# Feed-forward: weight conversions dealt over other steps, and accumulators evicted ahead of g's casts

## The chip, the cores and the metric

The kernel runs on one core of one Trainium2 chip. The metric is the device time of one execution in microseconds (us). Three runs of the kernel before took 407.21, 407.16 and 403.54 us; the median is 407.16.

## What is computed

Three layers follow each other: an attention with a local band and 32 global tokens (4 batches, 8 heads), a mixture of 8 experts with soft dispatch, and a feed-forward. The feed-forward, which the change touches, is

```
n_tokens, d_model, d_ff = (2304, 512, 2048)

def _moe2_ref(x, w_in, w_out) -> np.ndarray:
    h = x @ w_in
    g = h - np.tanh(h)
    return (g @ w_out).astype(np.float32)
```

Its input x is the output of the experts, a combination of 32 slots per token, so the kernel computes h from the combination weights and from a small matrix M (slots times w_in), with one matmul per 128 columns of d_ff. The weights w_in and w_out arrive as 64-bit words and are turned into 32-bit floats on the chip. The output has 17 tiles of 128 rows by 512 columns.

## The kernel before

**Steps.** The feed-forward is a list of 48 steps (L1116, from PHASES, L51). A step takes one chunk fc of 128 of the 2048 columns of d_ff and a group of six or five output tiles. The groups are tiles 0 to 5, 6 to 11 and 12 to 16; they are gone through with chunks 0 to 7 (steps 0 to 7, 8 to 15, 16 to 23) and then again with chunks 8 to 15 (steps 24 to 31, 32 to 39, 40 to 47). A sum over eight chunks is called a half: the accumulators of a group are evicted from PSUM once at the end of its first half (`keep_part`, L1178, on ScalarE) and once at the end of its second, where the two halves are added and written out (`emit_out`, L1184). A step of a group of five tiles (16 to 23 and 40 to 47) has 15 matmuls, the others 18.

**The matmuls of a step** (`ff`, L1167). Each tile takes three matmuls of 512 columns: the high half of g by the high half of the weight (L1174), the high half of g by the low half of the weight (L1175), the low half of g by the high half of the weight (L1176). So the second matmul of a step needs the low weight half `wlo[fc]` and the third the low half of g.

**g of a step, two steps ahead.** In step i the kernel makes g of step i + 2, in two parts (columns of the first three tiles, then of the others). One part goes from engine to engine:

- `g_head` (L1127): the h matmul on TensorE into one of two PSUM banks (L1133). The two banks take turns, so an h matmul must wait until the second tail of the part before the last has read its bank.
- `g_square` (L1138): u = h * h on ScalarE (L1140).
- `g_tail0` and `g_tail1` (L1144, L1148): two VectorE operations, h = (u - 2.5) * h (L1146), the first tail, and g = u * h (L1150), the second tail.
- `g_hi` (L1155): the high cast of g on ScalarE (L1157).
- `g_lo` (L1159): the low half, g minus its high cast, on GpSimd (L1161).

Each engine runs its instructions in the order in which the program issues them (`tc.manual_schedule`, L640). In the loop (L1332 to L1400) that order is, for part 0 and then part 1 of step i:

```
g_tail0(i + 2, part)
g_tail1(i + 2, part)
ff(i, tiles)
if part == 0: g_head(i + 2, 1); g_square(i + 2, 1)
if part == 0 and parts(i + 3) == 1: g_head(i + 3, 0); g_square(i + 3, 0)
g_hi(i + 2, part); g_lo(i + 2, part)
if part and parts(i + 3) > 1: g_head(i + 3, 0); g_square(i + 3, 0)
if last and i < len(steps) - 1: the evictions of the tiles of this part
```

So there is one h matmul in the middle of a step (for part 1 of step i + 2) and one at its end (for part 0 of step i + 3), and on ScalarE the high cast of part 0 stands behind the square of part 1. At the end of a half, in steps 7, 15 and 23, three evictions follow the high cast of part 0, and three (two) more follow the first square of the next step.

**Conversions.** A chunk of w_out (numbers 3 to 15) or w_in (numbers 24 to 31 stand for w_in's chunks 8 to 15) is turned from 64-bit words into floats by four operations: the head on ScalarE (`f32_head`, L531), then on VectorE the shift (L535), the high-word operation (L540) and the low-word operation (L545), from `f32_tail` (L533). A chunk of w_out then takes the high cast on ScalarE (L1036) and the low subtract on GpSimd (L1037), its low half. The chunks of w_out go through two conversion buffers in turn (`cv`, even and odd chunks), so the head of a chunk waits until the low subtract of the chunk two before it has read the buffer. `conv_ops` (L1026) gives a chunk's operations 0 to 5: nothing, shift, high-word, low-word, high cast, low subtract; `win_ops` (L618) gives the first four of a chunk of w_in.

**Where they stand before.** The table JOBS (L45) names the chunk of a step. Its head is issued in the middle of the step before (L1385 to L1391). Operation 1 follows the second tail of part 0, operation 2 the first tail of part 1, operation 3 the second tail of part 1 (L1342 to L1348), and operations 4 and 5 stand at the end of the step (L1398). Chunks 3 to 7 are converted in steps 1 to 5, each two steps ahead of the step that first uses it.

**M.** Two blocks of M are computed inside the loop, in steps 13 and 19 (MB, L49): `m_rows` (L1079) after the matmuls of part 0, `m_parts` (L1094) after those of part 1. Both take an h bank, so in these two steps the second h matmul takes the bank of the h matmul before it.

**Loads.** The raw chunks are loaded by `load_late` (L811), called at the top of each step (L1333) as long as a count that follows from JOBS allows and a buffer is free.

## Time and profile before

| What | Value |
|---|---|
| median of three runs | 407.16 us |
| the profiled execution | 406.85 us |
| its span, first to last instruction | 405.1 us |
| mean granted TensorE clock | 0.993 of full speed |
| TensorE busy | 382.9 us, 95% of the span |
| VectorE, ScalarE, GpSimd busy | 276.2, 218.2, 209.7 us |
| chain that ended last, on TensorE | 76% of the span |

A row of the timeline gives the start of an instruction in us from the start of the span, its duration in us, engine, line, operation, output <- input, shape, and in brackets how long its engine was idle before it and what ended that. PE is TensorE and PEld its weight loads, DVE VectorE, ACT ScalarE, POOL GpSimd. Matmuls overlap: from one start to the next is less than a duration. Names of buffers are of little use, since buffers are reused under old names (`slot`, `k_w`, `pg` are places in memory); the lines say what is done.

### The profile page before, as it was taken

Reading aid. Unit: us, or ns where it says so; the run is one execution under the profiler, and the core shown is the slowest. Engines: PE = TensorE matmul, PEld = TensorE weight load, DVE = VectorE, ACT = ScalarE, POOL = GpSimd, SP = SyncE. Lnnn points to the kernel's source line nnn. Section 1 sums busy time; section 2 is a strip of 40 time slices with the busy share of each in tenths; the row PEclk is TensorE's granted clock in tenths of the full one; section 3 lists DMA queues with packets and bytes.
Section 4 is the critical chain, followed back from the end, with each engine's and each line's share of the span. In section 5 each row is a group of like instructions: output and inputs, shape, how many; then the busy total and the mean of one; then the engine's idle time right before and its main releaser. Section 6 shows DMA issues by size and latency. Waiting matters only on the chain.

```text
span 405.1 us, 10230 instructions
## 1 busy us (share of the span) xinstructions
PE 382.9 (95%) x3767; PEld 279.6 (69%) x3767; DVE 276.2 (68%) x833; ACT 218.2 (54%) x542; POOL 209.7 (52%) x275
## 2 busy tenths in 40 slices
PE   7889889989999899999999999999989999999994
PEld 3677667766787433336877786786868888888873
DVE  4577698766476526449998886787879997555541
ACT  2677666865766202248655645566575645345330
POOL 3676576665564010016866444455575668347441
PEclk9999999999999999999999999999999999999998
DMA  6899999999768989999303101003100003002104
GB/s 182 264 401 317 321 335 268 357 334 294 266 183 270 332 254 418 416 420 385 111 0 105 53 1 53 0 4 94 60 2 2 0 28 129 0 2 113 44 2 138
DMA packets 33834, 70.43 MB, mean 174 GB/s; under 512 B 3824, under 2 KB 10736, under 8 KB 33776
## 3 DMA queue, kind: packets, MB, share of 16 engines
q1 hardware_dynamic: 33632, 69.56, 50.3%
q8 instruction: 32, 0.52, 0.5%
q14 instruction: 26, 0.21, 0.2%
q10 hardware_dynamic: 144, 0.13, 0.1%
HBM read 65.22 MB, written 4.46 MB: 172 GB/s over the span
## 4 chain that ended last, share of the span: by engine, by line
PE 76%; issue 6%; POOL 5%; DVE 4%; DMA 3%; ACT 3%; SPq 2%; DVEq 0%; POOLq 0%
PE a L1175 13%; PE a L1176 13%; PE a L1174 13%; PE sc L248 7%; PE a L971 4%; PE a L1010 4%; PE h L1133 4%; PE X L281 3%; PE ptp L269 3%; SPq L104 2%; PE gsc L430 2%; POOL q L210 2%; PE xTp L311 2%; PE ps L344 1%; DVE slot L1150 1%
## 5 line engine op out<-in xcount | busy, mean ns | idle before, releaser
L1161 POOL TENSOR_TENSOR slot<-slot 128x384 fp32r<-128x384 f32 x96 | 98.7, 1031 | 83.5 <-ACT slot L1157 79.8
L1174 PE MATMUL a<-slot 128*128 128x512 f32 x272 | 106.9, 393 | 1.3 <-ACT v_w L1182 0.7
L1176 PE MATMUL a<-slot 128*128 128x512 f32 x272 | 107.8, 396 | 0.0
L1175 PE MATMUL a<-slot 128*128 128x512 f32 x272 | 107.5, 395 | 0.0
L1146 DVE SCALAR_TENSOR_TENSOR h<-slot,h 128x384 f32<-128x384 f32 x96 | 51.5, 537 | 38.7 <-ACT slot L1140 38.4
L1157 ACT CAST slot<-slot 128x384 fp32r<-128x384 f32 x96 | 47.6, 496 | 49.5 <-DVE slot L1150 49.0
L1140 ACT ACTIVATE slot<-h 128x384 f32<-128x384 f32 x96 | 45.3, 473 | 34.5 <-PE h L1133 33.9
L1174 PEld LDWEIGHTS a<-slot 128*128 128x128 f32 x272 | 51.1, 188 | 14.2 <-ACT v_w L1182 1.5
L1176 PEld LDWEIGHTS a<-slot 128*128 128x128 f32 x272 | 51.0, 188 | 11.4
L1175 PEld LDWEIGHTS a<-slot 128*128 128x128 f32 x272 | 51.0, 188 | 9.3 <-POOL slot L1037 1.0
L1150 DVE TENSOR_TENSOR slot<-slot,h 128x384 f32<-128x384 f32 x96 | 50.8, 529 | 8.0 <-DVE h L1146 0.5
L258 ACT ACTIVATE sm<-sm,mb 128x128 f32<-128x128 f32 x128 | 41.2, 396 | 15.5 <-DVE mb L254 15.2
L248 PE MATMUL sc<-k,q 128*64 128x128 f32 x512 | 39.0, 294 | 4.9 <-POOL q L210 3.8
L210 POOL TENSOR_SCALAR v<-v 32x1300 f32<-32x1300 f32 (+5 forms) x40 | 34.2, 855 | 13.9 <-PE xgp L475 11.4
L248 PEld LDWEIGHTS sc<-k,q 128*64 128x64 f32 x512 | 33.3, 208 | 11.1 <-POOL q L210 5.9
L210 POOL TENSOR_SCALAR q<-q 64x256 f32<-64x256 f32 x62 | 27.5, 444 | 20.5 <-issue 11.0
L254 DVE CUSTOM_DVE_ANT_0 sm<-sc,mask 128x128 f32<-128x128 f32 x128 | 30.2, 284 | 10.9 <-PE sc L248 9.7
L1037 POOL TENSOR_TENSOR slot<-k_w,slot 128x512 fp32r<-128x512 f32 x16 | 20.7, 1296 | 32.5 <-ACT slot L1036 32.3
L1133 PE MATMUL h<-slot 128*128 128x384 f32 x96 | 32.4, 339 | 0.8 <-DVE slot L1150 0.6
L1133 PEld LDWEIGHTS h<-slot 128*128 128x128 f32 x96 | 17.9, 188 | 12.0 <-DVE slot L1150 5.9
L281 PE MATMUL X<-v,pt 128*32 128x65 f32 x1024 | 22.1, 223 | 1.4 <-issue 1.4
L281 PEld LDWEIGHTS X<-v,pt 128*32 128x32 f32 x1024 | 16.5, 109 | 7.2 <-issue 6.1
(239 smaller groups left out, 526.2 us busy)
## 6 DMA issues: line engine op xcount, KB each, us to landing
slot<-in_w_dram SPq DMA_DIRECT2D x55, 512.0 KB, 7.6
slot<-in_w_out_dram SPq DMA_DIRECT2D x9, 512.0 KB, 4.8
slot<-in_w_in_dram SPq DMA_DIRECT2D x16, 256.0 KB, 6.5
k<-in_k_dram SPq DMA_DIRECT2D x7, 576.0 KB, 7.8
q<-in_q_dram SPq DMA_DIRECT2D x15, 256.0 KB, 5.4
out_dram<-o SPq DMA_DIRECT2D x15, 256.0 KB, 2.1
slot<-in_w_in_dram SPq DMA_DIRECT2D x7, 512.0 KB, 10.0
v<-in_v_dram SPq DMA_DIRECT2D x8, 390.0 KB, 5.5
```

The costliest lines, as they stand in the source:

```text
L210: G.tensor_scalar(out=o, in0=i, scalar1=0.0, scalar2=1.0, op0=ALU.add, op1=ALU.mult)
L248: T.matmul(sc[64 * i:64 * i + 64, a, :], lhsT=q_b[2][:, 256 * i + jj:256 * i + 256:4], rhs=k[:, i, :, WINDOWS[t][jj][0]], skip_group_check ...
L281: T.matmul(X[32 * jj:32 * jj + 32, h, :], lhsT=pt[:, 128 * jj + 32 * h:128 * jj + 32 * h + 32], rhs=v[:, WINDOWS[t][jj][0], 65 * h:65 * h ...
L1133: T.matmul(h, lhsT=mst(128 * fc, 128), rhs=cst(128 * t0 + c.start, n))
L1140: S.activation(out=u, in_=h, func=AF.Square)
L1146: V.scalar_tensor_tensor(out=h, in0=u, scalar=-2.5, in1=h, op0=ALU.add, op1=ALU.mult)
L1150: V.tensor_tensor(out=g, in0=u, in1=h, op=ALU.mult)
L1157: S.copy(out=ghi, in_=g)
L1161: G.tensor_tensor(out=glo, in0=g, in1=ghi.bitcast(F32), op=ALU.subtract)
L1174: T.matmul(acc_t[j], lhsT=ghi[:, c], rhs=whi[fc], start=first, stop=False)
L1175: T.matmul(acc_t[j], lhsT=ghi[:, c], rhs=wlo[fc], start=False, stop=False)
L1176: T.matmul(acc_t[j], lhsT=glo[:, c], rhs=whi[fc], start=False, stop=last)
```

## The change

Three things are changed, all in the loop of the feed-forward.

1. JOBS puts some chunks in other steps: w_in's chunk 24 from step 7 to 8, 25 from 8 to 9, 28 from 13 to 12, w_out's chunks 8, 10 and 11 one step earlier (18, 21, 22).
2. A table PLACES says for each step and each of six places what is issued there: places 0 to 3 are those between and behind the tails, 4 the middle of the step, 5 its end. For chunks 3 and 4, and for all from 8 on, it gives the places of before. Chunk 5 is dealt over places (3, 1), (3, 3), (4, 0) and (4, 4), chunk 6 over (4, 2), (4, 3), (5, 1) and (5, 4), chunk 7 over (5, 3), (6, 0), (6, 1) and (6, 4): their high casts and low subtracts come half a step later, behind the casts and the low half of g's part 0.
3. The evictions at the end of a half come before the high cast of the part, and so before g_lo, the head and the first square of the next step.

```
@@ JOBS @@
-    1: 3, 2: 4, 3: 5, 4: 6, 5: 7, 7: 24, 8: 25, 10: 26, 11: 27, 13: 28, 14: 29, 16: 30, 17: 31,
-    19: 8, 20: 9, 22: 10, 23: 11, 25: 12, 26: 13, 28: 14, 29: 15,
+    1: 3, 2: 4, 3: 5, 4: 6, 5: 7, 8: 24, 9: 25, 10: 26, 11: 27, 12: 28, 14: 29, 16: 30, 17: 31,
+    18: 8, 20: 9, 21: 10, 22: 11, 25: 12, 26: 13, 28: 14, 29: 15,
+HEAD = -1
+PLACES = {
...
+    (4, 0): [(5, 3)], (4, 2): [(6, 0), (6, 1)], (4, 3): [(6, 2)], (4, 4): [(5, 4), (5, 5), (7, HEAD)],
...
+}
+for i, c in JOBS.items():
+    if c not in range(3, 8):
+        PLACES.setdefault((i - 1, 4), []).append((c, HEAD))
+        for k, p in enumerate((0, 1, 2, 3, 5, 5)):
+            PLACES.setdefault((i, p), []).append((c, k))
@@ new function @@
+        def place(i, p):
+            for c, k in PLACES.get((i, p), []):
+                if k == HEAD and c < 16:
+                    conv_head(c)
+                elif k == HEAD:
+                    win_room(c - 16)
+                    win_head(c - 16)
+                else:
+                    if k == 0:
+                        conv_t[c] = conv_ops(c) if c < 16 else win_ops(c - 16) + [lambda: None] * 2
+                    conv_t[c][k]()
@@ the loop @@
                 if part < parts(i + 2):
                     g_tail0(i + 2, part)
-                    for f in ops[2 * part:2 * part + 1]:
-                        f()
+                    place(i, 2 * part)
                     g_tail1(i + 2, part)
-                    for f in ops[2 * part + 1:2 * part + 2]:
-                        f()
+                    place(i, 2 * part + 1)
...
+                if last and i < len(steps) - 1:
+                    for j in tiles:
+                        (emit_out if fc == 15 else keep_part)(t0, j, -2.0 / 15.0)
                 if part < parts(i + 2):
                     g_hi(i + 2, part)
                     g_lo(i + 2, part)
                 if part == 0:
-                    c = JOBS.get(i + 1)
...
+                    place(i, 4)
                 if part and parts(i + 3) > 1:
                     g_head(i + 3, 0)
                     g_square(i + 3, 0)
-                if last and i < len(steps) - 1:
-                    for j in tiles:
-                        (emit_out if fc == 15 else keep_part)(t0, j, -2.0 / 15.0)
-            for f in ops[4:]:
-                f()
+            place(i, 5)
```

Two places show how the order on an engine moves. The first is GpSimd from chunk 4's low subtract to chunk 7's, in steps 2 to 6. The outputs slot_3184, slot_3180 and slot_3182 are the low halves of g, of steps 5, 6 and 7 in this order; slot_3364 to slot_3485 are the weight halves of chunks 4 to 7. Before:

```order
L1037 TENSOR_TENSOR slot_3364<-k_w_2326,slot_3364 128x512
L1161 TENSOR_TENSOR slot_3184<-slot_3178,slot_3183 128x384 x2
L1037 TENSOR_TENSOR slot_3405<-k_w_2326,slot_3405 128x512
L1161 TENSOR_TENSOR slot_3180<-slot_3178,slot_3179 128x384 x2
L1037 TENSOR_TENSOR slot_3446<-k_w_2326,slot_3446 128x512
L1161 TENSOR_TENSOR slot_3182<-slot_3178,slot_3181 128x384 x2
L1037 TENSOR_TENSOR slot_3485<-k_w_2326,slot_3485 128x512
```

After, with all line numbers 14 higher (L1051 is L1037, L1175 is L1161), and the weight halves of chunks 6 and 7 in slot_3462 and slot_3503:

```order
L1051 TENSOR_TENSOR slot_3365<-k_w_2326,slot_3365 128x512
L1175 TENSOR_TENSOR slot_3184<-slot_3178,slot_3183 128x384 x2
L1175 TENSOR_TENSOR slot_3180<-slot_3178,slot_3179 128x384
L1051 TENSOR_TENSOR slot_3405<-k_w_2326,slot_3405 128x512
L1175 TENSOR_TENSOR slot_3180<-slot_3178,slot_3179 128x384
L1175 TENSOR_TENSOR slot_3182<-slot_3178,slot_3181 128x384
L1051 TENSOR_TENSOR slot_3462<-k_w_2326,slot_3462 128x512
L1175 TENSOR_TENSOR slot_3182<-slot_3178,slot_3181 128x384
L1175 TENSOR_TENSOR slot_3184<-slot_3178,slot_3183 128x384
L1051 TENSOR_TENSOR slot_3503<-k_w_2326,slot_3503 128x512
```

Each low subtract of chunks 5, 6 and 7 now stands behind one more low half of g: chunk 5's, which was ahead of both parts of step 6's g, is between them.

The second place is ScalarE at the end of the first half, step 7 and the beginning of step 8. a0 to a5 are the accumulators, slot_3179 the high half of step 9's g, slot_3177 the squares. Before, from the square of part 1 of step 9:

```order
L1140 ACTIVATE slot_3177<-h_3572 128x384
L1157 CAST slot_3179<-slot_3178 128x384
L531 ACTIVATE pg_95<-slot_3444 128x512
L1182 ACTIVATE q_88<-a0_3265 128x512
L1182 ACTIVATE k_w_2629<-a1_3270 128x512
L1182 ACTIVATE q_88<-a2_3302 128x512
L1157 CAST slot_3179<-slot_3178 128x384
L1140 ACTIVATE slot_3177<-h_3596 128x384
L1182 ACTIVATE v_w_2699<-a3_3297 128x512
L1182 ACTIVATE slot_3600<-a4_3284 128x512
L1182 ACTIVATE slot_3600<-a5_3290 128x512
L1140 ACTIVATE slot_3177<-h_3618 128x384
```

After (L1196 is the eviction, L1171 the high cast, L1154 the square, L545 a head):

```order
L1154 ACTIVATE slot_3177<-h_3570 128x384
L1196 ACTIVATE q_88<-a0_3265 128x512
L1196 ACTIVATE pg_95<-a1_3270 128x512
L1196 ACTIVATE k_w_2326<-a2_3302 128x512
L1171 CAST slot_3179<-slot_3178 128x384
L545 ACTIVATE q_88<-slot_3439 128x512
L1196 ACTIVATE v_w_2469<-a3_3297 128x512
L1196 ACTIVATE slot_3591<-a4_3284 128x512
L1196 ACTIVATE slot_3591<-a5_3290 128x512
L1171 CAST slot_3179<-slot_3178 128x384
L1154 ACTIVATE slot_3177<-h_3596 128x384
L1154 ACTIVATE slot_3177<-h_3616 128x384
```

Each three evictions went from behind the high cast to ahead of it, and the second three from behind to ahead of the first square of step 10 (h_3596). The head between them is chunk 24's now, chunk 25's before.

## Rows read from the trace of the kernel before

**Rows 1.** Windows: engines' busy us (instructions), clock, DMA share, GB/s, 300 to 335 us

```profile
300.00:335.00 35.00, 35.00 (x156) 28.80 (x155) 30.99 (x52) 19.79 (x44) 23.16 (x22) 1.00 0.02 9
```

**Rows 2.** Waits of TensorE's weight loads, 186 to 400 us: total us, times, longest

```profile
PEld h L1133 <- DVE slot L1150: 4.4, 9, 1.1
...
PEld a L1175 <- POOL slot L1037: 1.0, 3, 0.4
```

**Rows 3.** Timeline of step 25 and the start of step 26

```profile
301.96 0.40 PE L1174 MATMUL a<-slot 128*128 128x512 f32 x1
...
304.06 0.33 PE L1133 MATMUL h<-slot 128*128 128x384 f32 x1
...
304.49 0.49 ACT L1140 ACTIVATE slot<-h 128x384 f32<-128x384 f32 x1 [1.35 <-PE h L1133]
...
304.88 0.51 ACT L1157 CAST slot<-slot 128x384 fp32r<-128x384 f32 x1
...
305.46 1.02 POOL L1161 TENSOR_TENSOR slot<-slot 128x384 fp32r<-128x384 f32 x1 [1.57 <-ACT slot L1157]
...
306.50 0.40 PE L1174 MATMUL a<-slot 128*128 128x512 f32 x1
```

**Rows 4.** Timeline: VectorE in step 3's program, chunk 5's low subtract, TensorE's step 5

```profile
204.23 0.55 DVE L1146 SCALAR_TENSOR_TENSOR h<-slot,h 128x384 f32<-128x384 f32 x1
...
207.81 1.30 POOL L1037 TENSOR_TENSOR slot<-k_w,slot 128x512 fp32r<-128x512 f32 x1
...
208.82 0.39 PE L1174 MATMUL a<-slot 128*128 128x512 f32 x1
```

**Rows 5.** Timeline of one step of VectorE with a conversion (w_in chunk 27)

```profile
239.61 0.56 DVE L1146 SCALAR_TENSOR_TENSOR h<-slot,h 128x384 f32<-128x384 f32 x1 [0.37 <-ACT slot L1140]
...
240.27 0.55 DVE L1150 TENSOR_TENSOR slot<-slot,h 128x384 f32<-128x384 f32 x1
...
241.46 1.01 POOL L1161 TENSOR_TENSOR slot<-slot 128x384 fp32r<-128x384 f32 x1 [1.18 <-ACT slot L1157]
241.55 1.47 DVE L540 SCALAR_TENSOR_TENSOR v_w<-slot,v_w 128x512 int32<-128x512 int32 x1
...
242.94 0.54 DVE L1150 TENSOR_TENSOR slot<-slot,h 128x384 f32<-128x384 f32 x1
...
243.51 0.52 ACT L1157 CAST slot<-slot 128x384 fp32r<-128x384 f32 x1 [2.13 <-DVE slot L1150]
243.93 0.48 ACT L1140 ACTIVATE slot<-h 128x384 f32<-128x384 f32 x1
...
244.45 0.56 DVE L1146 SCALAR_TENSOR_TENSOR h<-slot,h 128x384 f32<-128x384 f32 x1 [0.37 <-ACT slot L1140]
```

**Rows 6.** Timeline: first matmuls of steps 8 and 14, first tail of step 8

```profile
223.74 0.49 PE L1174 MATMUL a<-slot 128*128 128x512 f32 x1
...
225.71 0.56 DVE L1146 SCALAR_TENSOR_TENSOR h<-slot,h 128x384 f32<-128x384 f32 x1 [0.37 <-ACT slot L1140]
...
253.84 0.39 PE L1174 MATMUL a<-slot 128*128 128x512 f32 x1
```

**Rows 7.** The high-word operation by line: duration in ns, min/median/max, first and last start

```profile
L540 DVE SCALAR_TENSOR_TENSOR k_w<-slot,k_w x10: 693/1050/1546, 174.0 to 324.7; 128x512 int32<-128x512 int32 x10
```

**Rows 8.** Timeline: first matmuls of steps 16 and 20, first tail of step 16

```profile
262.73 0.40 PE L1174 MATMUL a<-slot 128*128 128x512 f32 x1
...
264.27 0.56 DVE L1146 SCALAR_TENSOR_TENSOR h<-slot,h 128x384 f32<-128x384 f32 x1 [2.16 <-ACT slot L1140]
...
279.92 0.40 PE L1174 MATMUL a<-slot 128*128 128x512 f32 x1
```

**Rows 9.** Timeline: evictions of step 23 and the first matmul of step 24

```profile
295.72 0.59 ACT L1182 ACTIVATE q<-a 128x512 f32<-128x512 f32 x1
...
296.21 0.59 ACT L1182 ACTIVATE pg<-a 128x512 f32<-128x512 f32 x1
...
296.37 0.50 PE L1174 MATMUL a<-slot 128*128 128x512 f32 x1 [0.60 <-ACT q L1182]
```

More of the change, by code (lines that the diff above doesn't have):

```diff
@@ L45 @@
 JOBS = {
-    1: 3, 2: 4, 3: 5, 4: 6, 5: 7, 7: 24, 8: 25, 10: 26, 11: 27, 13: 28, 14: 29, 16: 30, 17: 31,
-    19: 8, 20: 9, 22: 10, 23: 11, 25: 12, 26: 13, 28: 14, 29: 15,
-}
+    1: 3, 2: 4, 3: 5, 4: 6, 5: 7, 8: 24, 9: 25, 10: 26, 11: 27, 12: 28, 14: 29, 16: 30, 17: 31,
+    18: 8, 20: 9, 21: 10, 22: 11, 25: 12, 26: 13, 28: 14, 29: 15,
+}
+HEAD = -1
+PLACES = {
+    (1, 0): [(3, 0)], (1, 1): [(3, 1)], (1, 2): [(3, 2)], (1, 3): [(3, 3)], (1, 4): [(4, HEAD)], (1, 5): [(3, 4), (3, 5)],
+    (2, 0): [(4, 0)], (2, 1): [(4, 1)], (2, 2): [(4, 2)], (2, 3): [(4, 3)], (2, 4): [(5, HEAD)], (2, 5): [(4, 4), (4, 5)],
+    (3, 1): [(5, 0), (5, 1)], (3, 3): [(5, 2)], (3, 4): [(6, HEAD)],
+    (4, 0): [(5, 3)], (4, 2): [(6, 0), (6, 1)], (4, 3): [(6, 2)], (4, 4): [(5, 4), (5, 5), (7, HEAD)],
+    (5, 1): [(6, 3)], (5, 3): [(7, 0), (7, 1)], (5, 4): [(6, 4), (6, 5)],
+    (6, 0): [(7, 2)], (6, 1): [(7, 3)], (6, 4): [(7, 4), (7, 5)],
+}
[4 more added lines that the diff above has]
+            PLACES.setdefault((i, p), []).append((c, k))
 MB = {13: 3, 19: 4}
@@ L1222, in emit_out @@
                     DMA.dma_start(out=out[544 * b:544 * b + 32, :], in_=o[32 * b:32 * b + 32, :])
+        conv_t = {}
+        def place(i, p):
[9 more added lines that the diff above has]
+                    conv_t[c][k]()
         def flag_step(k):
@@ L1336, in band_attention_soft_moe_tanhshrink_kernel @@
                 continue
-            c = JOBS.get(i)
-            ops = [] if c is None else conv_ops(c) if c < 16 else win_ops(c - 16)
             half = (nt + 1) // 2
@@ L1385, in band_attention_soft_moe_tanhshrink_kernel @@
                 if part == 0:
-                    c = JOBS.get(i + 1)
-                    if c is not None and c < 16:
-                        conv_head(c)
-                    elif c is not None:
-                        win_room(c - 16)
-                        win_head(c - 16)
+                    place(i, 4)
                 if part and parts(i + 3) > 1:
```

## The prediction

> **What bounds the kernel now.** I read the windows first. From 300 to 335 us TensorE is busy all 35 us while VectorE has 31, ScalarE 20 and GpSimd 23 [rows 1]. So in the feed-forward, which alone is changed, the other engines cost nothing until TensorE must wait, and the most that a reordering can win is the sum of TensorE's waits. The view of waits names them: matmuls held for an h bank that VectorE had not read, or for a low weight half that GpSimd had not written [rows 2], and, in the timeline, for an accumulator that ScalarE had not evicted [rows 9]. The pace to hold against them: an undisturbed step of six tiles takes 306.50 - 301.96 = 4.53 us, and the nine matmuls up to its h matmul 304.06 - 301.96 = 2.10, so 0.233 each [rows 3]. The parts below count 4.5 us of waits that the change could win; so the question is rather what the new order makes late.
>
> How late the others are by nature is read in two places. The h matmul in the middle of a step, at 304.06, is followed by its square at 304.49 (+0.43), by the high cast of g's first part at 304.88 (+0.39: ScalarE has it behind the square), and by the low subtract on GpSimd at 305.46 (+0.58), which lasts 1.02 [rows 3]. So g_lo of part 0 ends 4.5 us after its step began, although nothing is behind there. And where VectorE is behind, a step with a conversion goes round in 244.45 - 239.61 = 4.84: first tail to second tail 0.66, the second part's second tail at 242.94, its high cast +0.57, the next square +0.42, the next first tail +0.52 [rows 5]. That is 0.31 more than TensorE's 4.53: conversion steps in a row put VectorE 0.31 further behind each, and a step without one lets it catch up.
>
> **Part A: chunks 5, 6 and 7 of w_out, steps 3 to 7.** Chunks 0 to 4 stand as before. On GpSimd the low half of chunk 5 moves behind g_lo of part 0 of step 4; the second matmul of step 5 needs it. Chunks 6 and 7 move likewise. Lower bound: it starts as g_lo ends, 1.0 after its start, and takes 1.30 [rows 4], so it ends 0.43 + 0.39 + 0.58 + 1.0 + 1.30 = 3.7 after the h matmul of the step before. From the second matmul of one step to its h matmul are 8 x 0.233 = 1.87. So one such wait follows the other after 1.87 + 3.7 = 5.57, where TensorE alone takes 4.53: 1.04 per chunk, three times, since the h matmul that starts each chain stands behind the wait before it.
> The first wait is longer, as VectorE is behind there. Up to the first tail of part 1 of step 3, at 204.23 [rows 4], the order is the old one. From there, with the spacings of rows 5 and 3: second tail 0.66, cast 0.57, square 0.42, first tail of step 4 0.52, second tail 1.06 (not 0.66, as chunk 5's last word operation stands between, 0.69 alone [rows 7] and starting before the tail has quite ended), cast 0.57, g_lo 0.58, low half 1.0 and 1.30: 6.7 in all, 210.9. The second matmul of step 5 wants it at 208.82 [rows 4] + 0.23, so this wait is 1.9. Then 210.95 + 5.57 = 216.5 and 222.1 for chunks 6 and 7; step 8 starts 4.30 later, at 226.4, before at 223.74 [rows 6]. Part A costs 2.65. Floor: 3 x 1.04 = 3.1 less the 1.3 that steps 5 to 7 waste now (14.9 from 208.82 to 223.74 for 3 x 4.53), +1.8. Ceiling: the head of chunk 7 shares a conversion buffer with chunk 5, so on ScalarE it waits too, with casts queued behind it; another 0.2 a chunk, +3.3.
>
> **Part B: evictions of step 7, and five conversions in steps 8 to 12.** Count from the second matmul of step 7. Its h matmul comes at 1.87, the square at 2.30, three evictions from 2.69 at 0.49 each [rows 9], the cast at 4.15, chunk 24's head at 4.56, three more evictions up to 6.6, a cast, and only then the square of step 8 at 7.0 and its first tail at 7.5. Step 8 starts at 4.30, so VectorE begins it 3.2 late; before, this square stood ahead of the second three evictions and the tail began at 225.71, 1.97 after 223.74 [rows 6]. A conversion step's last tail ends 3.88 after its first one began (242.94 + 0.54 - 239.61 [rows 5]), here at 11.4; the h matmul that needs this bank is due at 4.30 + 4.53 + 2.10 = 10.9. Wait: 0.5. Steps 9 to 12 convert too, at 4.84 against 4.53: 0.3 each, 1.25. In step 13 (M's block 3) the second h matmul uses the bank of part 0 of the same step, whose second tail ends at 7.5 + 5 x 4.84 + 1.21 = 32.9, while TensorE is there at some 31.8: 1.15. Against these 2.9 stand waits that go, for the evictions in step 8 and for chunk 28's tail in step 13, some 0.3 and 0.7. From step 8 to step 14 I get 32.0; before 253.84 - 223.74 = 30.1 [rows 6]. Part B costs 1.9; bounds -0.6 (VectorE catches up, the old waits go) and +2.9.
>
> B rests on one row: the high-word operation beside GpSimd's subtract takes 1.47, alone 0.69 [rows 5, 7], and GpSimd is ahead of it by 0.09. I take that as it stands. The Trainium skill (SBUF — State Buffer, "Who interferes with whom") says that a VectorE instruction with two SBUF inputs and a GpSimd instruction that reads SBUF contend, and that the one issued first holds the other off. The trace agrees as far as it goes: 1.47 is no more than 0.69 and what is left of 1.01. By that rule, were VectorE first, the round would be about 4.0 and B would end at its lower bound, -0.6; the sum would be 409.7.
>
> **Part C: evictions of step 15; chunks 30, 31 and 8 in steps 16 to 18.** Steps of five tiles take only about 15 x 0.233 + 0.3 = 3.8. Three more evictions ahead of its square put the first tail of step 16 from 264.27 to 1.45 later, 3.0 after 262.73 [rows 8]. Its second tail ends 1.21 later, at 4.2; the h matmul at the step's end is due at 3.6: 0.6, then 0.1 and 0.05, and in step 19 (M's block 4) the second h matmul waits some 0.8 where 0.3 is lost now. Part C costs 1.3; bounds -0.3 and +1.8.
>
> **Part D: steps 20 to 24.** Now 301.96 - 279.92 = 22.0 [rows 3, 8] for 4 x 3.8 + 4.53 = 19.7: 2.3 lost, much of it where step 24 waits for ScalarE's evictions at 296.37 [rows 9]. The change has them ahead and step 23 free of a conversion; but chunks 9, 10 and 11 now follow each other in steps 20 to 22, where VectorE's round, carried through in the same way, is 4.3 to 5 against 3.8. I get waits of 0.5, 0.7 and 0.6 for h banks and 21.5 in all: -0.5, between -2.3 and +1. The evictions of steps 31 and 39 cost nothing: nothing is converted there, so VectorE has room.
>
> **Sum.** 2.65 + 1.9 + 1.3 - 0.5 = 5.35. The profiled execution took 406.85 (its span 405.1, and 1.75 around it); 406.85 + 5.35 = 412.2. The runs' median, 407.16, is 0.3 above that execution, and the three runs lie 3.7 apart; a difference under 1%, some 4 us, can hardly be told from none.
>
> **Rivals.**
> *Only A is real.* VectorE catches up in B and C, the old waits of 0.6 there go, and D gives 0.5: 406.85 + 2.65 - 0.6 - 0.5 = 408.4. For it: VectorE is busy 31 of 35 us, not 35 [rows 1]. Against: the 4.84 of rows 5 has its gaps inside the chain.
> *Evicting ahead pays (not slower).* No accumulator is waited for any more: D gives its whole 2.3, B 0.6, and A stays at its floor: 406.85 + 1.8 - 0.6 - 2.3 = 405.7. It decides if the first tail of step 8 begins less than 2.7 after its step (10.9 - 3.88 - 4.30), so that no bank is late. For it: the evictions are the longest single waits [rows 9]. Against: the square moved behind them.
> *The low halves are in time.* Then A gives its 1.3 as well: 406.85 - 1.3 - 0.6 - 2.3 = 402.6, faster. Against it: rows 3, where g_lo alone ends as the next step starts, with nothing behind.
>
> **Chances.** The forecast 0.55 (409.5 to 415, four fifths of it above 411.2), only A 0.25, evicting ahead pays 0.12, in time 0.08. Faster by over 1% is the last and a little: 0.09. Slower is the forecast's upper part and what lies above it: 0.50. Within 1%: 0.41. The range goes from 405.5 (the second rival) to 415.5 (A at 3.3, B and C near their upper bounds); the last rival and a tenth above are left out.
>
> **What would show it.** Right: in the changed profile the weight loads of the second matmul in steps 5, 6 and 7 wait for GpSimd's subtract 1 us or more each, and step 8 starts 2 to 3 us later; VectorE begins step 8 about 3 us after TensorE; h matmuls of steps 9 to 13 and 16 to 19 wait for VectorE; step 24 waits no longer for an eviction. Wrong: if the low half of chunk 5 ends before step 5 begins, A falls; if the h matmuls of steps 9 to 18 wait for nothing, B and C fall.

## The result, and the profile after

The changed kernel takes 412.73 us (median of six runs, 407.36 to 413.62), the kernel before 406.77 beside it (six runs). The ratio is 1.0138, with a 95% interval of 1.0095 to 1.0182: slower by 5.6 us, between 3.9 and 7.4. The forecast was 412.2 us, with 405.5 to 415.5 as its range.

The sum behind that figure is checked in one profiled execution of each, where single steps can be compared. The changed one took 412.52 us (span 410.7). Its feed-forward, from the first matmul of step 0 to the last of step 47, lasts 404.61 - 183.85 = 220.76 us, before 399.20 - 185.88 = 213.32: 7.44 more, where the sum said 5.35. The attention and the experts ahead of it, which are not changed, took 2.03 less in this execution; that the totals, 412.2 and 412.52, come so close is luck. In twelve executions profiled for this study step 0 begins anywhere between 180.2 and 187.0 us, while an undisturbed step repeats within 0.03 us. Single costs are therefore read from the feed-forward's steps, and only verdicts on the whole from the times. All line numbers of the changed kernel from the feed-forward's operations on are 14 higher: L1188 to L1190 are the three matmuls, L1147 the h matmul, L1051 the low subtract of a weight, L1050 its high cast.

What TensorE's weight loads and matmuls wait for from 184 to 405 us (total us, times, longest), to be held against [rows 2]:

```profile
PEld h L1147 <- DVE slot L1164: 10.4, 17, 2.0
...
PEld a L1189 <- POOL slot L1051: 4.1, 3, 2.1
...
PE a L1189 <- POOL slot L1051: 3.0, 3, 1.8
...
PEld a L1188 <- ACT slot L1050: 0.7, 1, 0.7
...
PEld a L1190 <- POOL slot L1175: 0.5, 1, 0.5
```

The waits for VectorE's second tail went from 4.4 us in nine places to 10.4 in seventeen, those for the low subtract from 1.0 to 4.1; two are of a new kind, for a high cast of a weight (L1050) and for the low half of g (L1175).

**Steps 4 and 5 (part A).** The timeline from the end of step 4, all engines:

```profile
206.58 0.62 ACT L1050 CAST slot<-k_w 128x512 fp32r<-128x512 f32 x1
206.58 0.34 PE L1147 MATMUL h<-slot 128*128 128x384 f32 x1
...
207.25 0.50 PE L1188 MATMUL a<-slot 128*128 128x512 f32 x1 [0.33 <-ACT slot L1050]
207.31 1.02 DVE L554 SCALAR_TENSOR_TENSOR k_w<-slot,k_w 128x512 int32<-128x512 int32 x1
207.75 1.71 POOL L1051 TENSOR_TENSOR slot<-k_w,slot 128x512 fp32r<-128x512 f32 x1
...
209.51 0.50 PE L1189 MATMUL a<-slot 128*128 128x512 f32 x1 [1.76 <-POOL slot L1051]
...
210.94 0.63 PE L1188 MATMUL a<-slot 128*128 128x512 f32 x1
...
211.37 0.63 PE L1189 MATMUL a<-slot 128*128 128x512 f32 x1
211.80 0.63 PE L1190 MATMUL a<-slot 128*128 128x512 f32 x1
```

The first matmul of step 5 waits for chunk 5's high cast, the second for its low subtract, which takes 1.71 here instead of 1.30 [rows 4]. Behind the wait the matmuls start 0.43 apart (210.94, 211.37, 211.80), not 0.23 as in [rows 3]. The windows say why; columns as in [rows 1], the last but two is the granted clock:

```profile
202.22:207.25 5.03, 4.70 (x22) 3.56 (x21) 4.55 (x10) 2.98 (x6) 2.51 (x3) 1.00 0.00 0
207.25:210.50 3.25, 1.49 (x5) 1.04 (x6) 1.08 (x2) 1.01 (x3) 2.21 (x2) 1.00 0.00 0
210.50:213.90 3.40, 3.40 (x10) 2.69 (x9) 2.28 (x4) 1.56 (x5) 1.15 (x2) 0.51 0.08 7
```

TensorE was busy for 1.49 of 3.25 us, and in the 3.40 us behind it the granted clock is 0.51, which is the lower of its two levels (1.2 GHz) nearly throughout. Nine matmuls start in that stretch (its count of ten has one that was already running), where 3.40 / 0.233 = 14 to 15 would.

**Steps 8 to 24 (parts B, C and D).** First matmul of step 8 and VectorE's first tail there, the wait in step 13, the first matmul of step 14 (compare [rows 6]); the same of step 16 with its first h wait, and step 20's first matmul (compare [rows 8]); then two of step 23's last evictions, the h matmul at its end, and the first matmuls of steps 24 and 25 (compare [rows 9]):

```profile
226.31 0.40 PE L1188 MATMUL a<-slot 128*128 128x512 f32 x1
...
229.51 0.56 DVE L1160 SCALAR_TENSOR_TENSOR h<-slot,h 128x384 f32<-128x384 f32 x1 [3.46 <-ACT slot L1154]
...
255.03 0.44 PE L1147 MATMUL h<-slot 128*128 128x384 f32 x1 [1.13 <-DVE slot L1164]
...
258.41 0.40 PE L1188 MATMUL a<-slot 128*128 128x512 f32 x1
...
267.29 0.40 PE L1188 MATMUL a<-slot 128*128 128x512 f32 x1
...
270.31 0.56 DVE L1160 SCALAR_TENSOR_TENSOR h<-slot,h 128x384 f32<-128x384 f32 x1 [3.62 <-ACT slot L1154]
...
271.58 0.44 PE L1147 MATMUL h<-slot 128*128 128x384 f32 x1 [0.53 <-DVE slot L1164]
...
285.69 0.40 PE L1188 MATMUL a<-slot 128*128 128x512 f32 x1
...
301.65 0.61 ACT L1196 ACTIVATE q<-a 128x512 f32<-128x512 f32 x1
302.13 0.62 ACT L1196 ACTIVATE k_w<-a 128x512 f32<-128x512 f32 x1
...
302.17 0.44 PE L1147 MATMUL h<-slot 128*128 128x384 f32 x1 [0.38 <-DVE slot L1164]
302.45 0.40 PE L1188 MATMUL a<-slot 128*128 128x512 f32 x1
...
307.01 0.39 PE L1188 MATMUL a<-slot 128*128 128x512 f32 x1
```

VectorE begins step 8 3.20 us after TensorE and step 16 3.02 after it; step 24 no longer waits for an accumulator.

**Step 41, not foreseen.** GpSimd has two additions of `emit_out` for step 39 (L1225) ahead of the low half of g (the first of the three in the second row), and a weight load waits for that:

```profile
376.09 2.54 POOL L1225 TENSOR_TENSOR o<-o,slot 128x512 f32<-128x512 f32 x2
...
378.58 2.46 POOL L1175 TENSOR_TENSOR slot<-slot 128x256 fp32r<-128x256 f32 x3
...
379.37 0.19 PEld L1190 LDWEIGHTS a<-slot 128*128 128x128 f32 x1 [0.52 <-POOL slot L1175]
```

All twelve traces in one table, each stretch worked out from the first matmuls of its steps (us):

| Kernel | steps 0-7 | 8-13 | 14-19 | 20-24 | 25 to end | feed-forward | against before |
|---|---|---|---|---|---|---|---|
| before | 37.86 | 30.10 | 26.08 | 22.04 | 97.24 | 213.32 | |
| the changed kernel | 42.46 | 32.10 | 27.28 | 21.32 | 97.60 | 220.76 | +7.44 |
| e1, deal undone | 37.85 | 32.08 | 27.28 | 21.66 | 97.56 | 216.43 | +3.11 |
| e2, evictions alone | 37.88 | 30.37 | 26.97 | 20.78 | 97.57 | 213.57 | +0.25 |
| e3, deal alone | 43.03 | 30.10 | 26.06 | 22.03 | 97.28 | 218.50 | +5.18 |
| e4, jobs alone | 37.82 | 31.07 | 26.07 | 22.12 | 97.27 | 214.35 | +1.03 |
| e5, chunk 5 back | 39.17 | 32.08 | 27.27 | 21.66 | 97.61 | 217.79 | +4.47 |
| e6, low half last | 39.49 | 32.12 | 27.27 | 21.31 | 97.36 | 217.55 | +4.23 |
| e12, filled wait | 41.32 | 32.11 | 27.28 | 21.31 | 97.57 | 219.59 | +6.27 |
| e7, square first | 37.85 | 29.88 | 26.08 | 21.52 | 97.28 | 212.61 | -0.71 |
| e10, evictions ahead in step 23 | 37.85 | 30.11 | 26.10 | 20.77 | 97.24 | 212.07 | -1.25 |
| e11, three edits | 37.55 | 29.89 | 26.08 | 20.54 | 97.22 | 211.28 | -2.04 |

### The profile page after: what moved, and what is told of

Read it like the earlier page. It is cut to its first block, busy times and chain, and to the rows that moved or that the text cites. A ratio compares the mean times of both kernels' runs of the same rounds, so it can differ in the third digit from the quotient of the medians.

```text
span 410.7 us, 10229 instructions
## 1 busy us (share of the span) xinstructions
PE 384.4 (94%) x3767; PEld 280.0 (68%) x3767; DVE 274.0 (67%) x833; ACT 219.6 (53%) x542; POOL 211.1 (51%) x275
## 4 chain that ended last, share of the span: by engine, by line
PE 51%; POOL 15%; issue 13%; DMA 11%; DVE 5%; ACT 3%; SPq 1%; POOLq 0%; DVEq 0%; ACTq 0%
PE a L1190 8%; PE a L1189 8%; PE a L1188 8%; POOL slot L1175 8%; DMA slot<-in_w_dram 8%; PE sc L262 7%; PE X L295 3%; PE ptp L283 3%; PE h L1147 3%; POOL q L224 2%; PE gsc L444 2%; POOL slot L1051 2%; PE xTp L325 1%; DVE slot L1164 1%; DMA v<-in_v_dram 1%
## 5 line engine op out<-in xcount | busy, mean ns | idle before, releaser
L1175 POOL TENSOR_TENSOR slot<-slot 128x384 fp32r<-128x384 f32 x96 | 100.0, 1045 | 85.4 <-ACT slot L1171 82.4
L1190 PE MATMUL a<-slot 128*128 128x512 f32 x272 | 108.4, 399 | 0.1
L1188 PE MATMUL a<-slot 128*128 128x512 f32 x272 | 107.2, 394 | 0.3 <-ACT slot L1050 0.3
L1171 ACT CAST slot<-slot 128x384 fp32r<-128x384 f32 x96 | 48.0, 500 | 53.2 <-DVE slot L1164 52.4
L1154 ACT ACTIVATE slot<-h 128x384 f32<-128x384 f32 x96 | 44.8, 477 | 37.4 <-PE h L1147 37.2
L1188 PEld LDWEIGHTS a<-slot 128*128 128x128 f32 x272 | 51.5, 189 | 12.4 <-ACT slot L1050 0.7
L1190 PEld LDWEIGHTS a<-slot 128*128 128x128 f32 x272 | 51.3, 189 | 12.0 <-POOL slot L1175 0.5
L224 POOL TENSOR_SCALAR v<-v 32x1300 f32<-32x1300 f32 (+5 forms) x40 | 34.0, 849 | 14.3 <-PE xgp L489 10.4
L1051 POOL TENSOR_TENSOR slot<-k_w,slot 128x512 fp32r<-128x512 f32 x16 | 21.2, 1326 | 33.7 <-DMA slot<-in_w_dram 24.9
L1147 PE MATMUL h<-slot 128*128 128x384 f32 x96 | 33.9, 355 | 3.5 <-DVE slot L1164 3.0
L1147 PEld LDWEIGHTS h<-slot 128*128 128x128 f32 x96 | 18.1, 189 | 16.5 <-DVE slot L1164 11.9
L283 PE MATMUL ptp<-ident,sm 128*128 128x128 f32 x128 | 21.0, 286 | 0.7 <-ACT pt L285 0.7
```

What stands on the lines that cost most here:

```text
L224: G.tensor_scalar(out=o, in0=i, scalar1=0.0, scalar2=1.0, op0=ALU.add, op1=ALU.mult)
L1147: T.matmul(h, lhsT=mst(128 * fc, 128), rhs=cst(128 * t0 + c.start, n))
L1154: S.activation(out=u, in_=h, func=AF.Square)
L1171: S.copy(out=ghi, in_=g)
L1175: G.tensor_tensor(out=glo, in0=g, in1=ghi.bitcast(F32), op=ALU.subtract)
L1188: T.matmul(acc_t[j], lhsT=ghi[:, c], rhs=whi[fc], start=first, stop=False)
```

## The experiments

**The parts one at a time.** Four kernels: the change without its deal, and before with one of the three parts each.

`e1_deal_undone`:

```
-PLACES = {
...
+PLACES = {}
 for i, c in JOBS.items():
-    if c not in range(3, 8):
+    if i > 1:
         PLACES.setdefault((i - 1, 4), []).append((c, HEAD))
...
```

> The changed kernel with chunks 5, 6 and 7 of w_out converted at the places of before; the other two edits stay. Theory (the late low halves cost part A, and the half clock after the first of these waits is their consequence): no wait of a second matmul above 0.2 us in steps 5 to 7, the granted clock 1.00 all through them, steps 0 to 7 take 37.9 us from first matmul to first matmul of step 8 as before (changed kernel: 42.5), B, C and D stay, so some 2.0 to 3.0 us above the kernel before and 4 to 5 below the changed one: about 409. Rival (the evictions ahead of the casts, or the clock dropping for another reason, make step 5 long): steps 0 to 7 still take over 40 us and the time stays above 411.

Measured: 408.49 us (ten runs), ratio 1.0080 [1.0043, 1.0117]. Steps 0 to 7 take 37.85 as before; the rest is as in the changed kernel (32.08, 27.28, 21.66). So the deal of three chunks costs what it costs in steps 0 to 7. (Step 24 takes 4.90 here and in e5, 4.56 in the changed kernel, e6 and e12; what decides that was not followed up.)

`e2_evict_alone`:

```
+                if last and i < len(steps) - 1:
+                    for j in tiles:
+                        (emit_out if fc == 15 else keep_part)(t0, j, -2.0 / 15.0)
                 if part < parts(i + 2):
                     g_hi(i + 2, part)
```

> The kernel before with nothing changed but the evictions ahead of the high casts. Theory (the evictions only hurt where conversion steps follow each other, and help step 24): first tail of step 8 some 3.2 us after TensorE's step 8 instead of 2.0, an h wait of about 0.5 in step 9, none in steps 10 to 12 (step 9 converts nothing), steps 16 to 19 0.8 longer, steps 23 and 24 1.0 to 2.0 shorter: within 1 us of the kernel before. Rival (evicting ahead is by itself the loss of steps 8 to 19): 2 to 3 us above the kernel before.

Measured: 405.65 us (ten runs), ratio 0.9999 [0.9951, 1.0047]. The feed-forward is 0.25 longer: 0.27 lost in steps 8 to 13, 0.89 in steps 14 to 19, 0.33 at step 41, and 1.26 won in steps 20 to 24. A gain and three losses that cancel.

`e3_deal_alone`:

```
+    (3, 1): [(5, 0), (5, 1)], (3, 3): [(5, 2)], (3, 4): [(6, HEAD)],
+    (4, 0): [(5, 3)], (4, 2): [(6, 0), (6, 1)], (4, 3): [(6, 2)], (4, 4): [(5, 4), (5, 5), (7, HEAD)],
...
```

> The kernel before with only chunks 5, 6 and 7 dealt as in the change. Theory (part A, clock included): steps 0 to 7 take 42 to 42.5 us against 37.9, a stretch of some 3.4 us at a granted clock of 0.5 after a wait of 1.8 us or more in step 5, steps 8 to 47 as in the kernel before: 4 to 4.6 us above it. Rival (the half clock was an accident of one execution): waits only, 2.65 us above the kernel before and the clock at 1.00.

Measured: 408.99 us (four runs), ratio 1.0102 [1.0015, 1.0189]. Steps 0 to 7 take 43.03, 5.17 more than before, all else is as before. Step 5 takes 8.19, in the changed kernel 8.21. The clock falls here too, but sooner behind the wait. The first stretch below answers to that of the changed kernel, the second is the one at the lower clock:

```profile
205.97:209.22 3.25, 1.48 (x4) 1.02 (x5) 1.10 (x2) 1.00 (x3) 2.21 (x2) 0.90 0.00 0
208.55:211.95 3.40, 3.40 (x10) 2.68 (x9) 1.72 (x3) 1.12 (x3) 1.00 (x1) 0.50 0.00 0
```

The difference to the changed kernel, 5.17 against 4.60, lies in step 6 (5.81 against 5.19). Here the slow stretch is over soon after step 5's h matmul, which starts the chain of chunk 6's low half at 211.57; the nine matmuls behind it run at full clock and then wait 1.02 us for that half. In the changed kernel the slow stretch covers the first of these matmuls (its h matmul starts at 212.22), and the wait is 0.41.

`e4_jobs_alone`:

```
-    1: 3, 2: 4, 3: 5, 4: 6, 5: 7, 7: 24, 8: 25, 10: 26, 11: 27, 13: 28, ...
+    1: 3, 2: 4, 3: 5, 4: 6, 5: 7, 8: 24, 9: 25, 10: 26, 11: 27, 12: 28, ...
```

> The kernel before with only the table JOBS of the change. Theory (each conversion step without a pause puts VectorE 0.31 us further behind; here it starts step 8 only 2.0 behind): no h wait in steps 8 and 9, waits of 0.1 to 0.3 in steps 11 to 13 and about 1 us for the second h matmul of step 13, and steps 20 to 24 no shorter than before: 0.5 to 2.0 us above the kernel before. Rival (evictions ahead, not the run of conversions, bring the lag): no h wait in steps 8 to 13 beyond those of before, time within 0.5 us of it.

Measured: 406.37 us (ten runs), ratio 1.0026 [0.9991, 1.0062]. Five conversions in a row cost 0.97 in steps 8 to 13, where the evictions alone cost 0.27; both together (e1) cost 1.98. The run of conversions alone is late for the h banks from step 11 on (steps 11, 12 and 13 take 4.67, 4.87 and 7.86, before 4.53, 4.53 and 7.14); when it also starts late, steps 9 and 10 wait as well (4.92 and 4.81 in e1): 0.74 of part B belongs to neither edit alone. In times of the whole, this kernel and the one before are not told apart.

**Why part A was larger than its sum.** Two kernels take the long wait away in different ways, a third keeps it and fills it.

`e5_chunk5_back`:

```
-    (3, 1): [(5, 0), (5, 1)], (3, 3): [(5, 2)], (3, 4): [(6, HEAD)],
-    (4, 0): [(5, 3)], (4, 2): [(6, 0), (6, 1)], (4, 3): [(6, 2)], (4, 4): [(5, 4), (5, 5), (7, HEAD)],
+    (3, 1): [(5, 0), (5, 1)], (3, 2): [(5, 2)], (3, 3): [(5, 3)], (3, 4): [(6, HEAD)], (3, 5): [(5, 4), (5, 5)],
+    (4, 2): [(6, 0), (6, 1)], (4, 3): [(6, 2)], (4, 4): [(7, HEAD)],
```

> The changed kernel with the operations of chunk 5 alone back at their old places (its shift word after the second tail of step 3's second half, its last two at the end of step 3); chunks 6 and 7 stay dealt, and the jobs and the evictions ahead stay. Theory (long wait, then half clock): of the 5.17 us that the dealt chunks cost, step 5 holds 3.1, because its low half came 1.76 us late and TensorE's granted clock then fell to 0.51; with chunk 5 in time there is no fall, steps 4 and 5 take 4.6 and 5.1 as before, steps 6 and 7 show waits of about 0.5 to 1.0 each for the low halves of chunks 6 and 7, and the eight steps 0 to 7 last 38.5 to 39.8 us (37.86 before, 43.0 with all three dealt); the feed-forward is 3.7 to 5.0 us longer than before instead of 7.4, the time about 409.5 to 411. Rival 1 (the load of VectorE and GpSimd in these steps, wherever chunk 5 goes, makes the fall): a granted clock near 0.5 to 0.8 in step 6 or 7, steps 0 to 7 over 41 us. Rival 2 (chunks 6 and 7 were only late because step 5 had pushed all of it): no waits at steps 6 and 7, 37.9 us.

Measured: 409.98 us (six runs), ratio 1.0098 [1.0059, 1.0137]; steps 0 to 7 take 39.17, steps 4 to 7 4.55, 4.77, 5.80 and 5.67. The two waits that are left, in the timeline, and the stretch with the first of them, in the windows:

```profile
209.32 0.50 PE L1189 MATMUL a<-slot 128*128 128x512 f32 x1 [1.02 <-POOL slot L1051]
...
214.98 0.51 PE L1189 MATMUL a<-slot 128*128 128x512 f32 x1 [0.87 <-POOL slot L1051]
```

```profile
207.91:211.00 3.09, 2.07 (x9) 1.44 (x9) 3.09 (x5) 0.90 (x2) 2.51 (x3) 1.00 0.58 175
211.00:213.71 2.71, 2.71 (x13) 2.22 (x13) 2.16 (x4) 1.64 (x4) 1.04 (x2) 1.00 0.27 30
```

Both rivals fall: a wait of 1.02 leaves the clock at 1.00, and chunks 6 and 7 are late by themselves. Chunk 5 alone makes 42.46 - 39.17 = 3.29 of the 4.60.

`e6_lowlast`:

```
+            for j, c in cs:
+                T.matmul(acc_t[j], lhsT=ghi[:, c], rhs=whi[fc], start=first, stop=False)
+            for j, c in cs:
+                T.matmul(acc_t[j], lhsT=glo[:, c], rhs=whi[fc], start=False, stop=False)
+            for j, c in cs:
+                T.matmul(acc_t[j], lhsT=ghi[:, c], rhs=wlo[fc], start=False, stop=last)
```

> The changed kernel with another order of the same matmuls: in every step but the first of a group of banks, a half's tiles do all products with the high part of w_out, of both parts of g, ahead of all products with its low part, so that the low half is wanted six matmuls (about 1.37 us) later than now (it was wanted by the second). Theory (the low half's lateness is the whole cost of the dealt chunks, the fall of the clock its second part): the wait of step 5 shrinks from 1.76 to about 0.4 or less, those of steps 6 and 7 (0.41 and 0.88) vanish, no fall of the granted clock; what is left in step 4 and 5 is the wait of 0.33 to 0.5 for the high half's cast; steps 0 to 7 last 38 to 39 us (42.45 in the changed kernel, 37.86 before), the feed-forward is 2.5 to 4 us longer than before instead of 7.4, the time 409 to 410. Rival (the low part of g, which GpSimd makes last, is wanted earlier by this order, and now comes too late in every step): new waits for it of up to 0.3 us in each of some 80 halves, the feed-forward longer than that of the changed kernel, time over 415.

Measured: 410.18 us (six runs), ratio 1.0081 [1.0037, 1.0126]; steps 0 to 7 take 39.49, 0.5 us over the upper figure expected, and the feed-forward is 4.23 longer, 0.2 over it. The granted clock stays at 1.00. Three of the waits left in steps 5 and 6, in this kernel's timeline (L1195 is the first product, L1199 the one with the low half; x3 is three matmuls in a row):

```profile
207.72 0.97 PE L1195 MATMUL a<-slot 128*128 128x512 f32 x3 [0.27 <-ACT slot L1050]
...
210.00 0.97 PE L1199 MATMUL a<-slot 128*128 128x512 f32 x3 [0.61 <-POOL slot L1051]
...
213.98 0.96 PE L1195 MATMUL a<-slot 128*128 128x512 f32 x3 [0.57 <-ACT slot L1050]
```

What had not been expected is the last row: with the low half out of the way, the high cast is late in step 6 too. The rival falls: the low part of g, wanted earlier, is in time (steps 8 to 24 take what they took).

`e12_fill`, with seven more products in step 5, whose sums the reference does not have:

```
                 T.matmul(acc_t[j], lhsT=ghi[:, c], rhs=whi[fc], start=first, stop=False)
+                for _ in range(7 if i == 5 and j == tiles[0] and j == tile_order(t0, nt)[0] else 0):
+                    T.matmul(acc_t[j], lhsT=ghi[:, c], rhs=whi[fc], start=False, stop=False)
```

> The changed kernel with seven more matmuls in step 5: its first product of the high parts is repeated seven times into the same bank (seven times 0.23 us = 1.6 us), so that TensorE works where it waited 1.76 us for the low half of w_out's chunk 5. What this adds to one tile's sums is work that the reference does not have. Theory (the idle stretch lets the granted clock fall, and the fall alone costs about 1.7 us behind it): no stretch of step 5 below a clock of 0.9; the second matmul still starts when the low half is there, but the following 3.4 us hold some 14 matmuls instead of 10; step 5 takes 6.4 to 6.8 us instead of 8.21, the feed-forward is about 1.6 us shorter than the changed kernel's (5.6 to 6.0 us longer than before). Rival (the 3.4 us behind the wait are slow for another cause, operands or banks that come late): step 5 takes 8.2 us or more, the feed-forward 7.4 us longer than before or worse.

Measured: 411.76 us (four runs), ratio 1.0166 [1.0086, 1.0247]. The timeline of the wait, and the windows of step 5:

```profile
206.73 1.76 PE L1190 MATMUL a<-slot 128*128 128x512 f32 x7
208.69 0.50 PE L1191 MATMUL a<-slot 128*128 128x512 f32 x1 [0.20 <-POOL slot L1051]
```

```profile
206.40:209.65 3.25, 3.05 (x12) 2.25 (x13) 1.09 (x2) 0.98 (x3) 2.24 (x2) 1.00 0.00 0
209.65:213.08 3.43, 3.43 (x17) 2.81 (x16) 2.71 (x6) 2.01 (x5) 2.09 (x3) 1.00 0.05 6
```

The low half comes as late as before (2.29 us after the step's first matmul, in the changed kernel 2.26), but the clock stays at 1.00, 15 matmuls start in the next 3.43 us instead of nine in 3.40, and step 5 takes 6.68 instead of 8.21. The rival falls: what is slow behind the wait is the clock, and it goes with TensorE standing idle. Both profiled executions with the wait of 1.76 or 1.77 have the fall (the changed kernel and e3), the four in which the wait is undone, shortened or filled do not (e1, e5, e6, e12). It need not come in every execution: in one of the six of the changed kernel (407.36 us) the mean granted clock was 0.997, which leaves some 0.003 x 405.6 = 1.2 us for all falls together, and this one alone would take 3.40 x 0.49 = 1.67. In the traces the fall costs 1.53 in step 5. Of that 0.43 comes back in step 6 (5.62 here, 5.19 in the changed kernel), since a slow TensorE wants chunk 6's low half later; in e3, where the fall lies earlier, nothing comes back. In the feed-forward it is 7.44 - 6.27 = 1.17, less than the 1.6 expected. The time of the whole, over four runs, does not tell the two kernels apart.

**Is there a better kernel?** Three edits of the kernel before, two alone and then all together.

`e7_square_first` (the first half's square ahead of the second half's cast):

```
+                if part and parts(i + 3) > 1:
+                    g_head(i + 3, 0)
+                    g_square(i + 3, 0)
                 if part < parts(i + 2):
                     g_hi(i + 2, part)
```

> The kernel before with two things of each step exchanged: the first half's head and square of g for three steps on are issued ahead of the cast and subtract of the second half's g, instead of behind them, so that VectorE's second operation of that half does not wait for ScalarE's square behind the cast. Theory (in a step with a conversion VectorE's round of 4.5 to 4.8 us is what TensorE's product with w_in waits for): these waits of the kernel before, 4.4 us in nine places in the feed-forward, shrink by about the 0.37 us each that VectorE stands idle in such a round, the feed-forward becomes 0.5 to 2.5 us shorter, 404 to 406 us. Rival (the cast of the second half's g, now behind the square of 0.5 us, comes too late for the half's first matmul): steps of 4.53 us grow to 4.7 or more, the feed-forward longer by 2 us or more, 408 us or above.

Measured: 404.75 us (ten runs), ratio 0.9981 [0.9940, 1.0022]; the feed-forward is 0.71 shorter, 0.22 of it in steps 8 to 13 and 0.52 in steps 20 to 24. No step grows but step 24 (5.68 instead of 5.60, behind a step 23 that is 0.45 shorter), so the rival falls. The times of the whole do not tell the two kernels apart.

`e10_evict23` (e2's edit with `if i == 23`, the others behind as before):

> The kernel before with the evictions ahead of g's two parts in step 23 alone, behind them in steps 7, 15, 31 and 39 as before. Theory (evicting ahead pays where the next group of banks waits for these evictions, costs where VectorE or GpSimd are the later ones): steps 23 and 24 take 4.22 and 5.07 as in the run with all evictions ahead (4.99 and 5.59 before), with none of its losses at steps 8 and 9 (0.35), 16 to 18 (0.95) and 41 (0.35); the feed-forward is 1.2 to 1.4 us shorter than before, time about 405. Rival (the gain at step 24 came only because GpSimd and VectorE were already later from step 16 on): steps 23 and 24 take 10.6 together as before, no change of the feed-forward.

Measured: 405.77 us (ten runs), ratio 0.9940 [0.9898, 0.9983]; steps 23 and 24 take 4.22 and 5.06, the feed-forward is 1.25 shorter, and the losses of e2 are gone. (1.25 us is 0.3% of the whole; the rest of the 0.6% is scatter of the executions.) The end of step 23 and the first matmul of step 24 in the timeline, with the third of the last evictions:

```profile
296.51 0.44 PE L1133 MATMUL h<-slot 128*128 128x384 f32 x1 [0.16 <-DVE slot L1150]
296.79 0.39 PE L1174 MATMUL a<-slot 128*128 128x512 f32 x1
...
296.94 0.62 ACT L1182 ACTIVATE k_w<-a 128x512 f32<-128x512 f32 x1
```

What step 24 still waits for is VectorE, not ScalarE: its first matmul starts before the third eviction does.

`e11_three` (e7, e10 and e6's order of matmuls):

> The kernel before with three small edits together: the evictions ahead in step 23 alone (by itself 1.25 us less in the feed-forward), the first half's square of three steps on ahead of the cast of the second half's g (by itself 0.70 us less), and the products with the low part of w_out last in a half (it took the waits for low halves of some 0.5 us each from steps 5 and 6 and a part of that of step 7 in the changed kernel). Theory (they act on different waits): steps 5, 6 and 7 take 14.0 to 14.6 us together instead of 14.92, the feed-forward is 2.3 to 3.2 us shorter than before, the time 403 to 404, ratio 0.992 to 0.994. Rival (the first two share step 24's slack, and the third has nothing to take, since VectorE's round of 4.8 to 5.1 us with a conversion keeps the product with w_in as long): 1.2 to 1.6 us shorter, ratio 0.996 to 0.997.

Measured: 403.71 us (twelve runs), ratio 0.9953 [0.9922, 0.9984], faster than both kernels, if by little. The feed-forward is 2.04 shorter, between theory and rival: the first two edits give 1.71 together (0.71 and 1.25 alone), the third only 0.31, most of it (0.23) in step 7. Steps 5 and 6 still take 5.07 and 5.04; what ends their waits is VectorE's round, as the rival said.

## Why the prediction was right, and where its sum was wrong

**What it had right.** The sign and the mechanism: the low halves of chunks 5, 6 and 7 came late, each start of a group began with VectorE behind, and step 24's accumulator wait went. Part B gave 32.10 us from step 8 to 14 (32.0 forecast), with its 3.2 of lateness and the wait of 1.13 in step 13 (1.15 forecast). Part C cost 27.28 - 26.08 = 1.20 (1.3), the first tail of step 16 being 3.02 late (3.0). Part D gave 0.72 back (0.5), from step 20 to 25 21.32 us (21.5); a third of a microsecond of that, in step 24, is not explained (e1 and e5 lack it). Together these are 0.4 us off. The rule of the Trainium skill that was weighed in part B (SBUF — State Buffer, "Who interferes with whom": a VectorE operation with two SBUF inputs and a GpSimd operation hold each other off, the earlier one first) would have changed the sum only if VectorE had come first there. It did not; in steps 8 to 12 the high-word operation is second and stretched, as before:

```profile
236.21 1.01 POOL L1175 TENSOR_TENSOR slot<-slot 128x384 fp32r<-128x384 f32 x1 [1.18 <-ACT slot L1171]
236.30 1.47 DVE L554 SCALAR_TENSOR_TENSOR k_w<-slot,k_w 128x512 int32<-128x512 int32 x1
```

**The step that failed is the size of part A:** 4.60 (42.46 - 37.86) where the prediction wrote 2.65, above its ceiling of 3.3. Its term of 1.04 for a chunk was nearly right: chunks 6 and 7 alone (e5) make steps 6 and 7 1.27 and 1.14 longer than 4.53. Two things were missing. The larger is the clock: a wait of 1.76 was priced at what it lasts, and it cost 1.17 beyond that (e12). The other is the low subtract, put at 1.30 from a row where nothing stretches it; it took 1.71, so chunk 5's low half was ready 7.24 us after step 4 began (209.46 - 202.22), not 6.7. The rest of its chain came as forecast to 0.1. In e12, where only the fall of the clock is gone, steps 4 to 7 take 4.97, 6.68, 5.62 and 5.67, where the prediction's working gives 4.58, 6.43, 5.57 and 5.57: 0.79 more, of which the stretched subtract is 0.41. The prediction also followed only the low subtract. The high cast stands in the same place, behind the cast of g, and step 5's first matmul waits for it, so that step 4 takes 5.03 instead of 4.58; but this adds nothing to the sum here, since the second matmul would have waited for the low half all the same. It counts once the low half is out of the way (e6).

**What no term held:** the evictions of steps 31 and 39 were to cost nothing, since nothing is converted there. Those of step 39 do not only occupy ScalarE: `emit_out` brings GpSimd's additions, which now stand ahead of the low half of g (0.35 at step 41). That they are the cause is read from the row and from e2, which has the same wait without any other edit; e10, which leaves step 39 as it was, does not have it.

**The rivals.** "Only A is real" falls with e1, which has everything but A and is 3.11 longer in the feed-forward. "Evicting ahead pays" falls for all groups together (e2, +0.25), but holds for the end of the third group alone (e10, -1.25). Why there is argued, not shown: in that kernel chunk 11 is still converted in step 23, but step 24 converts nothing, while conversions stand in step 8 and in steps 16 and 17, behind the other two first halves. "The low halves are in time" falls with e3.

**The expected gain.** The change meant three gains: no waits for low halves, none for accumulators, none for the tails of conversions. The second was real, 1.26 us. The other two were turned into longer waits for the same engines: for the low halves since their new places come behind the casts and a low half of g on engines that run in order (e3), for the tails since five conversions now follow each other (e4) and VectorE begins them later (e2).

## What to carry to other kernels

Ahead of moving an operation to a later place on an in-order engine, list everything that the moved group makes (here a high cast and a low subtract) and the instruction that wants each first; the output that comes latest against its reader sets the price, and the next one takes its place when that is mended (e6). Moving evictions ahead can pay at one place and cost at another, so try it group by group: all five ends together gave nothing, one of them 1.25 us. And a wait on TensorE that is long against the work around it may cost more than its length, since the granted clock can fall behind it: look at the window after the wait as well.

## What the runs showed of the hardware that was not expected

The granted clock fell to 0.51 for some 3.4 us after TensorE had been busy 1.49 of 3.25 us, with 1.76 as the longest idle stretch; with 2.07 busy of 3.09 (e5) and with 3.05 of 3.25 (e12) it stayed at 1.00. The fall came in both executions profiled with all three chunks dealt and the wait left as it was. What decides between these cases was not tried.

The low subtract on GpSimd is stretched by a VectorE operation on a weight that began ahead of it. The sixteen of a kernel by line, duration in ns (min/median/max, first and last start), before and after:

```profile
L1037 POOL TENSOR_TENSOR slot<-k_w,slot x16: 1268/1298/1315, 176.1 to 327.8; 128x512 fp32r<-128x512 f32 x16
```

```profile
L1051 POOL TENSOR_TENSOR slot<-k_w,slot x16: 1267/1292/1707, 172.3 to 332.8; 128x512 fp32r<-128x512 f32 x16
```

The one of 1.71 is chunk 5's in the timeline of step 5. It began while the high-word operation (L554, both inputs in SBUF) had 0.58 us to run; 0.58 shared, 0.41 lost. Chunk 6's took 1.48: it began while the shift (L549, one input) had 0.33 to run, and lost 0.2. In e3 the same two take 1.71 and 1.45.

```profile
214.44 0.61 DVE L549 TENSOR_SCALAR k_w<-k_w 128x512 int32<-128x512 int32 x1
214.72 1.48 POOL L1051 TENSOR_TENSOR slot<-k_w,slot 128x512 fp32r<-128x512 f32 x1
```

In the kernel before, tails of VectorE run beside nearly all of these subtracts and none takes over 1.32 us. Shifts run beside nine of the sixteen too, but each begins behind the subtract, and then the shift is the one that is stretched, here beside the subtract of [rows 4] (a shift beside no GpSimd operation takes 0.42):

```profile
208.32 1.08 DVE L535 TENSOR_SCALAR k_w<-k_w 128x512 int32<-128x512 int32 x1
```

So for both operations the one that comes second is the longer. For the high-word operation, with [rows 5], where VectorE came second and was stretched, this agrees with the same section of the Trainium skill from the other side as to which of the two is held off; the loss, 0.41, is less than the time shared.
